# A fused attention and mixer kernel: float32 first tiles, another order of the opening, and four GpSimd sums per unit

## The chip, the core and the metric

The kernel runs on one core of a Trainium2 chip. The metric is the time of one execution on the device, in microseconds (us). Engines are named as in the profile: PE is TensorE, PEld its weight loads, DVE VectorE, ACT ScalarE, POOL GpSimd, SP the engine that issues the DMAs. "L615" is line 615 of the kernel before.

## What is computed

The input x has 2048 rows of 512 numbers. It is normalized, and the result goes two ways: through a sliding, dilated attention (32 heads of 16 numbers; each position looks at itself and at the seven positions 2, 4, ... 14 rows back), and through a two-layer network with GELU, whose output passes SiLU. The product of the two ways is added to x:

```python
xn = _layernorm(x)
qkv = (xn @ wqkv)                      # q, k, v: 32 heads of 16
idx = pos[:, None] - 2 * arange(8)     # window of 8, dilation 2
logits = einsum("bhsd,bhswd->bhsw", q, k[idx]) * 16 ** -0.5   # idx < 0 masked
s = einsum("bhsw,bhswd->bhsd", softmax(logits), v[idx]) @ wo
y = _layernorm(xn)
g = silu(gelu(y @ w1 + b1) @ w2 + b2)  # w1 512 x 1376, w2 1376 x 512
out = x + s * g
```

All is float32 in and out.

## The kernel before

**Layout.** Even and odd rows never meet in the attention (dilation 2), so they are two classes (c = 0, 1) of 1024 rows, each in eight tiles of 128 rows. A class has four blocks of eight heads (hb = 0 to 3). That makes eight units u of attention, in the order c = 0 with hb 0 to 3, then c = 1.

**Precision.** A float32 matrix product is made of three fp16 ones: each operand is scaled by a power of two and split into a high part and a low part (what the rounding left), and high x high, low x high and high x low are summed in PSUM. The scale comes from a sum of squares of the weights (ScalarE with accumulation, L458 for wqkv and L376 for w1 and wo; a matmul with a tile of fours sums it over the partitions, L384 or L389, `total`; VectorE makes the power of two from the exponent, L402 to L413). The high part is ScalarE's (L476, L429) or VectorE's (L427), the low part VectorE's (L478, L430).

**Opening (`ln0`, L531; `prep_q`, L453).** The even tiles are loaded in the order of `LOADS` (tiles 2, 3, then the first weight block in two DMAs, "q0" and "q2", then 0-1, 4-5, 6-7), normalized (statistics on VectorE L518, a power on GpSimd L505 and L512, the scaling on VectorE L554 or ScalarE L527), transposed on TensorE (L561) into PSUM, and split from there into yT (high on ScalarE L565, low on VectorE L566). Sixteen matmuls on constants (L1000, the count is `WAKE`) fill gaps of TensorE behind the first normalized tile.

**Projection (`qkv`, L595).** Per unit eight tiles of 12 fp16 matmuls (L615) into one of two PSUM buffers "ps"; ScalarE evicts each (L623) with its row scale (cs) into the unit's tile U[u % 2], which holds q, k and v of eight tiles plus copied halo rows of k and v (DMAs, L632 and L638). U is double-buffered over units, so the projections of unit u + 1 write where unit u - 1 was.

**Attention (`attention`, L651), VectorE above all.** Four products of q with shifted k (L666, 128 x 2048 each, into a ring of three buffers "prod"), each followed by a reduction over the 16 numbers of a head (L669); softmax (L689 to L697, exp on ScalarE L692); four products of the weights with shifted v (L722). The PV products acc, p1, p2, p3 are summed: two VectorE additions of 2048 (acc + p1, acc + p2, L717), then three GpSimd additions of 1024 (`beside`, L742), which are handed over in the list `pend` and taken out in the next unit's loop over the q-k products, at n = 1, 2 and 3. Each has a one-element copy ahead (L745) that waits for a q-k product, so that the addition (L746) runs beside the reduction of it. Then the result is split into fp16 (L705, L707), transposed by DMA (L710) into oT.

**Network (`mlp1`, L848; `mlp2`, L892).** 44 steps (four chunks of 512 rows x 11 blocks of w1): 12 matmuls (L856), GELU on ScalarE (L873), the high part on ScalarE (L876). The low part is VectorE's (L879) for steps in `DVE_LO` (8 to 43); for steps 0 to 7 a matmul with a negative diagonal subtracts the high part in PSUM (L885) and ScalarE reads the rest (L888). Two steps later 12 matmuls with w2 (L901) add to four z buffers.

**End (`wo_first` L796, `wo_last` L814).** Output projections (L792): for odd rows nine matmuls per tile over the first three head blocks, three more when the last block's oT is there; then the scaling and product with g (L836), the addition of x (L783 on VectorE, L785 on GpSimd) and the store (L786).

**Order.** Nothing runs in the order in which the code names it. Every operation goes into a list with an estimated duration, its reads and writes and a priority (`Plan.add`); `Plan.issue` (L201) plays the engines through with these estimates and so fixes each engine's order; the engines then execute in that order and wait on semaphores. DMAs are modelled with a rate, an issue time and a tail; up to the time `SLOW` a lower rate is taken. `port=True` marks operations that the plan lets use the port that VectorE and GpSimd share only one after the other. Lower priority numbers go first: projections of unit u have 1000 u, network steps 1000000 and above, so the network fills what the projections leave. `qkv(u + 1)` is put on the list ahead of `attention(u)` (L1135 to L1139).

## Time and profile before

| what | value |
|---|---|
| median of three runs (lowest to highest) | 424.1 us (423.76 to 425.4) |
| the profiled execution | 424.13 us |
| its span in the trace | 422.4 us |
| TensorE busy, matmuls | 408.6 us, 2098 |
| VectorE busy | 391.8 us |
| ScalarE busy | 215.7 us |
| GpSimd busy | 78.2 us |
| first projection matmul (L615) | 11.8 us |
| first network matmul (L856) | 49.9 us |
| end of the last matmul | 417.8 us |

The execution's own time is longer than the span by 1.7 us, which lie around it. A line of the timeline gives the start, the length of a merged group, engine, line, operation and tiles, the count, and in brackets the idle time before it with what ended it. A line of the stretches gives, for each engine, the busy time and the number of instructions in parentheses, then the granted TensorE clock, the share of the DMA engines and GB/s.

### The profile page before, as it was taken

To read this page: it belongs to the slowest core of one execution; us is meant where nothing else is said; L and a number is where in the kernel's file an instruction comes from. 1 tells how busy PE (TensorE), PEld (TensorE's weight loads), DVE (VectorE), ACT (ScalarE), POOL (GpSimd) and SP (SyncE) were. 2 spreads that over 40 slices of the span, in tenths; PEclk is the share of its full clock that TensorE was granted. 3 is DMA by queue.
4 is the path that set the end of the run, shared out by engine and by line. 5 is a ranking of instruction groups with operands and counts; after the bars stand their busy time and mean duration, and the time that the engine had idled before them with its cause. 6 is when DMAs were issued, how large, how long until landed. Compare 5 with 4: busy or idle time off the path is not lost.

```text
span 422.4 us, 5540 instructions
## 1 busy us (share of the span) xinstructions
PE 408.6 (97%) x2098; PEld 208.2 (49%) x2098; DVE 391.8 (93%) x400; ACT 215.7 (51%) x325; POOL 78.2 (19%) x119
## 2 busy tenths in 40 slices
PE   4999989999999999999999999999999999999995
PEld 3565534445644564445544554455545554444442
DVE  4985999999998999999999999998999989999974
ACT  3899974872477754833375352234230492236400
POOL 5310200000450023202500240052002500250022
PEclk9999999999999999999999999999999999999999
DMA  7964260120044347430262022110425374007142
GB/s 259 415 267 137 69 218 2 67 82 2 1 122 166 68 102 170 92 58 2 72 164 100 0 88 50 52 66 36 136 75 175 74 219 143 2 0 222 37 138 101
DMA packets 42506, 44.83 MB, mean 106 GB/s; under 512 B 27464, under 2 KB 27648, under 8 KB 41968
## 3 DMA queue, kind: packets, MB, share of 16 engines
q1 hardware_dynamic: 42480, 44.49, 34.7%
q8 instruction: 16, 0.26, 0.2%
q14 instruction: 10, 0.08, 0.1%
HBM read 23.53 MB, written 7.34 MB: 73 GB/s over the span
## 4 chain that ended last, share of the span: by engine, by line
PE 85%; DVE 6%; ACT 4%; DMA 3%; issue 1%; SPq 0%; POOL 0%; DVEq 0%
PE z L901 27%; PE mh L856 25%; PE ps L615 22%; PE ps L792 6%; PE z L792 2%; DVE w L430 2%; DMA prod<-in_A_wqkv_dram 1%; PE mh L792 1%; DMA yT<-in_A_wqkv_dram 1%; DVE bn L518 1%; ACT w L376 1%; DMA U<-U 1%; ACT wq L458 1%; ACT U L623 1%; ACT yT L565 1%
## 5 line engine op out<-in xcount | busy, mean ns | idle before, releaser
L615 PE MATMUL ps<-wq,yT 128*128 128x384 f16 x768 | 130.0, 326 | 0.7 <-ACT U L623 0.7
L856 PE MATMUL mh<-yT,w 128*128 128x512 f16 (+1 forms) x528 | 121.3, 379 | 0.1
L901 PE MATMUL z<-w,h 128*128 128x512 f16 x480 | 111.5, 379 | 0.0
L615 PEld LDWEIGHTS <-yT 128*128 128x128 f16 x768 | 75.1, 98 | 52.2 <-issue 2.1
L856 PEld LDWEIGHTS <-w 128*128 128x128 f16 (+1 forms) x528 | 52.8, 100 | 60.9 <-issue 0.4
L873 ACT ACTIVATE mh<-mh,b1T,hsc 128x512 f32<-128x512 f32 (+1 forms) x44 | 33.0, 750 | 89.9 <-PE mh L856 89.8
L666 DVE TENSOR_TENSOR prod<-U 128x2048 f32<-128x2048 f32 x32 | 73.0, 2287 | 1.1 <-DMA U<-U 0.4
L901 PEld LDWEIGHTS <-h 128*128 128x128 f16 x480 | 47.0, 98 | 54.8
L669 DVE TENSOR_REDUCE L<-prod 128x128 f32<-128x2048 f32 x32 | 72.8, 2280 | 0.2
L623 ACT ACTIVATE U<-ps,cs 128x384 f32<-128x384 f32 x64 | 37.0, 583 | 64.3 <-PE ps L615 64.1
L722 DVE TENSOR_TENSOR prod<-L,U 128x2048 f32<-128x2048 f32 x28 | 63.1, 2284 | 0.2
L745 POOL COPY gate<-prod 1x1 f32<-1x1 f32 x21 | 4.4, 212 | 242.1 <-DVE prod L666 210.0
L717 DVE TENSOR_TENSOR prod<-prod,prod 128x2048 f32<-128x2048 f32 x16 | 36.5, 2284 | 0.0
L746 POOL TENSOR_TENSOR prod<-prod 128x1024 f32<-128x1024 f32 x14 | 32.9, 2351 | 0.0
L792 PEld LDWEIGHTS <-oT 128*128 128x128 f16 x192 | 18.8, 98 | 22.6
L876 ACT ACTIVATE h<-mh,hsc 128x512 f16<-128x512 f32 x40 | 27.5, 686 | 0.9
L792 PE MATMUL ps<-wo,oT 128*128 128x512 f16 x120 | 27.2, 379 | 0.0
L879 DVE SCALAR_TENSOR_TENSOR h<-mh,hsc,h 128x512 f16<-128x512 f32 x32 | 23.7, 742 | 2.3 <-ACT h L876 2.3
L746 POOL TENSOR_TENSOR prod<-prod,prod 128x1024 f32<-128x1024 f32 x7 | 16.4, 2348 | 0.0
L705 ACT ACTIVATE o<-prod,osc 128x1024 f16<-128x1024 f32 (+1 forms) x9 | 9.5, 1051 | 11.3 <-POOL prod L746 5.8
L873 ACT ACT_TABLE_LOAD x10 | 12.8, 1283 | 0.2
L561 PE MATMUL z<-ident,f 128*128 128x128 f32 x32 | 6.0, 318 | 6.6 <-DVE f L554 5.9
(146 smaller groups left out, 332.8 us busy)
## 6 DMA issues: line engine op xcount, KB each, us to landing
f<-in_A_x_dram SPq DMA_DIRECT2D x31, 256.0 KB, 4.4
U<-U SPq DMA_DIRECT2D x16, 392.0 KB, 3.6
gd<-f SPq DMA_DIRECT2D x12, 256.0 KB, 2.5
oT<-in_B_w_dram SPq DMA_DIRECT2D x2, 1024.0 KB
yT<-in_B_w_dram SPq DMA_DIRECT2D x2, 1024.0 KB, 13.3
f<-gd SPq DMA_DIRECT2D x8, 256.0 KB, 3.2
out_dram<-f SPq DMA_DIRECT2D x8, 256.0 KB, 2.1
out_dram<-U SPq DMA_DIRECT2D x8, 256.0 KB, 2.0
```

Of the source, the lines that this page charges most:

```text
L615: nc.tensor.matmul(b.t[:, 0:384], y[:, s, k, o:o + P], wq[:, hb, t, k], start=(n == 0), stop=(n == 11))
L623: act(384, lambda i=i, b=b: nc.scalar.activation(U3[:, i:i + 31:15, :], b.t[:, 0:384].rearrange("p (t e) -> p t e", t=3), AF.Identity, sca ...
L666: dve(2048, lambda p2=p2, g=g: nc.vector.tensor_tensor(p2(), q, slots(Ut, KH, 2 * g), op=ALU.mult), qk + [("kh", ub, 0), ("kh", ub, 1), (" ...
L669: dve(2048, lambda pr=pr, g=g: nc.vector.tensor_reduce(L3()[:, 2 * g:2 * g + 2], pr.t.rearrange("p (r f d) -> p r f d", r=2, d=DH), AX.X, ...
L717: dve(n, lambda: nc.vector.tensor_tensor(d(), a(), b(), op=ALU.add), keys, [dkey])
L722: dve(2048, lambda: nc.vector.tensor_tensor(pr.t.rearrange("p (r f d) -> p r f d", r=2, d=DH), L3()[:, 2 * g:2 * g + 2].rearrange("p r (f ...
L746: nc.gpsimd.tensor_tensor(x.t[:, 0:1024], x.t[:, 0:1024], y(), op=ALU.add)
L792: nc.tensor.matmul(b.t, oT[:, hb, i // 4, s, i % 4], wo[:, t, hb], start=(hb == 0 and n == 0), stop=(hb == NHB - 1 and n == 2))
L856: nc.tensor.matmul(b.t[0:M], w1[:, s, k, f * P:f * P + M], yT[ch][:, t, k], start=(n == 0), stop=(n == 11))
L873: act(512, lambda: nc.scalar.activation(b.t[0:M], b.t[0:M], AF.Gelu_apprx_tanh, bias=b1T[0:M, f:f + 1], scale=hsc[0:M, 1:2]), [b, ("b1T",) ...
L876: act(512, lambda: nc.scalar.activation(hi()[0:M], b.t[0:M], AF.Identity, scale=hsc[0:M, 2:3]), [b], [hk])
L901: nc.tensor.matmul(z.t, hl[s][0:K, t * P:(t + 1) * P], w2[0:K, w, f], start=(f == 0 and n == 0), stop=(f == NF - 1 and n == 2))
```

## The change

- **Loads.** Tile 3 is loaded after the first weight block in place of before it.
- **Float32 first tiles.** For tiles 2 and 3 (`FP`) of unit 0, ScalarE first copies the transposed tile from PSUM to a float32 tile yF. The projection of these two tiles is four float32 matmuls of 384 columns on yF and the raw weights, in place of twelve fp16 ones; the row scale loses the weight scale. The fp16 high and low parts, which other units and the network read, are made from yF at a lower priority.
- **PSUM.** In unit 0, and for the first four tiles of unit 1, every second projection tile takes a buffer of the ring "mh".
- **Idle matmuls.** 22 without any input, and 4 behind the first normalized tile, in the buffer z0, in place of 16 in "mh".
- **PV sums (units 0 to 6).** The third PV product is written over the unit's own q and k slots (the first 2048 columns of U). VectorE adds only its first half to acc (1024 in place of 2048); the second half is added on GpSimd to p3, by a fourth `beside` entry. The four entries are taken out at n = 0, 1, 2 and 3 of the next unit.
- **Order of the list.** `qkv(u + 1)` is put on the list inside `attention(u)`, after its first q-k product and the first GpSimd addition (`mid`), since it overwrites the tile that this addition reads.
- **Network.** `DVE_LO` begins at step 4, so steps 4 to 7 lose the subtraction matmul and ScalarE's L888 and get VectorE's L879.
- **End.** The last tile's three matmuls, scaling, addition and store are done in two halves of 256 columns; its addition moves no engine (VectorE).
- **Estimates of the planner.** `SLOW` 5.5 for 7.8; a tail of 3.5 for the DMAs of weight blocks 2 and 3 (1.4 before); priorities `PQLO` and `PFP`; GpSimd's additions 2.2 for 2.45; the powers on GpSimd without the port.

```diff
-LOADS = [(2, 1), (3, 1), "q0", "q2", (0, 2), (4, 2), (6, 2)]
+LOADS = [(2, 1), "q0", "q2", (3, 1), (0, 2), (4, 2), (6, 2)]
+FP = (2, 3)
-DVE_LO = range(8, 44)
+DVE_LO = range(4, 44)
-SLOW = 7.8
+SLOW = 5.5
-WAKE = 16
+WAKE = 4
+WAKE0 = 22
-PQLO = 0.45
+PQLO = 0.55
+PFP = 0.62
+U1MH = 4
...
     def k0(hb):
-        return dict(rate=400e3, tail=0.6, issue=0.45) if hb == 0 else {}
+        return dict(rate=400e3, tail=0.6, issue=0.45) if hb == 0 else dict(tail=3.5) if hb > 1 else {}
...
-            act(512, lambda p3=p3, hi=hi: nc.scalar.copy(hi, p3()), [b], [("yh", 0, i)], aps=0, **way)
+            if i in FP:
+                yf = yF[i] = R_L.new()
+                act(512, lambda b=b, yf=yf: nc.scalar.copy(yf.t, b.t), [b], [yf], aps=0, **way)
+                p3, b, way2 = (lambda yf=yf: yf.t.rearrange("p (k t) -> p k t", k=KT)), yf, dict(prio=PFP)
+            else:
+                way2 = way
+            act(512, lambda p3=p3, hi=hi: nc.scalar.copy(hi, p3()), [b], [("yh", 0, i)], aps=0, **way2)
             dve(512, lambda p3=p3, hi=hi, lo=lo: nc.vector.tensor_tensor(
-                lo, p3(), hi, op=ALU.subtract), [b, ("yh", 0, i)], [("y", 0, i)], port=False, **way)
+                lo, p3(), hi, op=ALU.subtract), [b, ("yh", 0, i)], [("y", 0, i)], port=i in FP, **way2)
...
-        for i in IORD if u else IORD0:
+        for n, i in enumerate(IORD if u else IORD0):
+            more = n % 2 and (u == 0 or u == 1 and n < U1MH)
...
-            b = R_ps.new()
+            b = (R_mh if more else R_ps).new()
...
-            ends = [1, 2, 3, 4, 8, 12] if u == 0 and i == IORD0[0] else [4, 8, 12] if u < 2 else [12]
+            ends = [4, 8, 12] if u < 2 else [12]
+            if u == 0 and i in FP:
+                yf = yF[i]
+                for k in range(KT):
+                    pe(1, 384, lambda k=k, b=b, yf=yf: nc.tensor.matmul(
+                        b.t[:, 0:384], yf.t[:, k * P:(k + 1) * P], stq[hb]()[:, k * 384:(k + 1) * 384],
+                        start=(k == 0), stop=(k == KT - 1)), [yf, ("stq", hb, k)], [b], fp32=4.1,
+                       holds=stkey[hb], after=pl.users([b] + [("v", ub, i)]))
+                ends = []
...
-            if pend and n:
+            if pend:
                 pend.pop(0)(pr)
                 if n == 3:
                     pend.pop(0)()
+            if n == 0:
+                mid()
...
             acc = pv(0)
             p1 = pv(1)
-            p2 = pv(2)
-            addto(acc, p1)
+            pv(2, p2t)
+            add(2048, lambda: acc.t, lambda: p1.t, lambda: acc.t, [acc, p1], acc)
             p3 = pv(3)
-            addto(acc, p2)
+            add(1024, lambda: acc.t[:, 0:1024], lambda: p2t[:, 0:1024], lambda: acc.t[:, 0:1024], [acc] + qkk, acc)
...
-            pend.extend([beside(acc, lambda: acc.t[:, 1024:2048]),
-                         beside(p3, lambda: p3.t[:, 1024:2048]),
-                         beside(acc, lambda: p3.t[:, 0:1024]), rest])
+            pend.extend([beside(p3, lambda: p2t[:, 1024:2048], qkk),
+                         beside(acc, lambda: acc.t[:, 1024:2048], []),
+                         beside(p3, lambda: p3.t[:, 1024:2048], []),
+                         beside(acc, lambda: p3.t[:, 0:1024], []), rest])
...
+            if i == NI - 1:
+                for h in range(2):
+                    cols = slice(h * 256, h * 256 + 256)
...
-    for _ in range(WAKE):
-        b = R_mh.new()
+    for n in range(WAKE0 + WAKE):
+        b = R_z[0].new()
         pl.add("pe", 0.2, lambda b=b: nc.tensor.matmul(b.t[:, 0:2 * P], idle[:, 0:P], idle, start=True,
-                                                       stop=True), [("yd", 2)], [b], prio=1e9)
+                                                       stop=True), [("yd", 2)] if n >= WAKE0 else [], [b], prio=1e9)
...
-        if 2 <= u + 1 < len(units):
-            with prio(PR_U * (u + 1)):
-                qkv(*units[u + 1], u + 1)
+        def mid():
+            if 2 <= u + 1 < len(units):
+                with prio(PR_U * (u + 1)):
+                    qkv(*units[u + 1], u + 1)
         with prio(PR_U * (u + 1) + 500):
-            attention(c, hb, u)
+            attention(c, hb, u, mid)
```

## The prediction

> **What bounds the kernel now.** I read the busy row of each engine, then the chain of work that ended last, then the waits, then the stretches. First the page, then four stretches of the span (TensorE's columns are the first after the length):
>
> ```profile
> PE 408.6 (97%) x2098; PEld 208.2 (49%) x2098; DVE 391.8 (93%) x400; ACT 215.7 (51%) x325; POOL 78.2 (19%) x119
> ...
> PE 85%; DVE 6%; ACT 4%; DMA 3%; issue 1%; SPq 0%; POOL 0%; DVEq 0%
> ```
>
> ```profile
> 0.00:11.80 11.80, 5.79 (x27) 4.53 (x28) 6.43 (x28) 4.57 (x9) 5.58 (x16) 1.00 0.80 276
> 11.80:49.90 38.10, 36.66 (x229) 22.25 (x227) 31.08 (x81) 36.32 (x67) 7.32 (x7) 1.00 0.57 214
> 49.90:60.10 10.20, 8.53 (x40) 3.61 (x37) 10.20 (x12) 6.75 (x12) 0.00 (x0) 1.00 0.86 281
> 60.10:417.80 357.70, 357.62 (x1806) 177.78 (x1806) 342.68 (x281) 168.10 (x241) 65.28 (x96) 1.00 0.30 84
> ```
>
> From 60.1 us to 417.8 us TensorE is busy 357.62 of 357.70 us. In that stretch the end moves only if TensorE is given less work or starts it sooner; time taken off VectorE, ScalarE or GpSimd there is worth nothing by itself. What can be won lies ahead of 60 us (no projection before 11.8 us, then 1.4 and 1.7 us of idle), and in the 4.6 us behind the last matmul.
>
> TensorE's timeline of the opening and of its one long wait:
>
> ```profile
> 5.88 1.12 PE L561 MATMUL z<-ident,f 128*128 128x128 f32 x4 [5.88 <-DVE f L554]
> 6.79 1.06 PE L1000 MATMUL mh<-fours 128*128 128x256 bf16 x4
> ...
> 12.36 2.89 PE L615 MATMUL ps<-wq,yT 128*128 128x384 f16 x15
> 15.55 0.66 PE L561 MATMUL z<-ident,f 128*128 128x128 f32 x4 [0.31 <-ACT f L527]
> ...
> 57.75 0.81 PE L856 MATMUL mh<-yT,w 128*128 128x512 f16 x3
> 60.14 0.38 PE L384 MATMUL ps<-s,fours 128*128 128x1 f32 x2 [1.58 <-ACT wq L458]
> ```
>
> The first projection matmuls wait for the prepared fp16 weights: ScalarE's sum of squares starts at 6.99 us, when the raw weights land, the scale comes from VectorE at 10.6 us, the first fp16 weights after that. At 58.5 us TensorE's queue holds the "total" of the third weight block (L384), whose data landed only at 59.1 us; TensorE stands for 1.58 us behind it while gelu tiles for L901 are ready (ScalarE finished the first at 55.5 us).
>
> **The change, part by part.** All is counted against the profiled execution: 424.13 us, of which the span is 422.4; its median over three runs is 424.1 us, so the two agree.
>
> *Float32 first tiles.* Tiles 2 and 3 of the first unit lose 24 fp16 matmuls and get 8 fp32 ones that read the raw weights. An fp16 matmul of 384 columns costs 1.95/12 = 0.1625 us (the chain's "1.95 PE ps L615 x12"), so the old 24 cost 3.9 us, and their evictions ended at 19.1 us. For an fp32 matmul of this size there is no row. Bounds: as fast as fp16, 0.65 us a tile; or the slow transposes at 5.88 us, 1.12/4 = 0.28 us for 128 columns, three times that for 384 and four of them, 3.4 us. I take the fp32 transposes once TensorE is at speed (0.66/4 for 128 columns): 2.0 us a tile. Either way they run while TensorE had nothing to do but idle matmuls (L1000), so only a late end would cost. They can start when the fp32 copy of the transposed tile is out: transposes end near 6.5, the raw weights land near 6.4 (their DMAs now stand one 0.43 us issue earlier, ahead of tile 3's), ScalarE first does a 0.94 us sum, then the copy (0.48): about 7.9 us. Tile 3 now lands behind the weights (near 7 us), its normalization, transposes and copy take it to about 11, so both tiles are done near 13.5 us instead of 18.4. That is 4.9 us at most.
> The Trainium skill ("FP8 and Floating Point Precision", "TensorE Precision Notes") says that true FP32 is four passes through the array. Worked out from the row of fp16, that is an estimate of 4 x 4 x 0.1625 = 2.6 us a tile; the sum would stay the same, since tile 3 arrives later than that. No row here shows an fp32 matmul of this size.
>
> How much of the 4.9 us stays? Behind it lie two chains. Tiles 0, 1, 4 to 7 still come from VectorE and ScalarE (their transposes run from 15.6 to 24.9 us), so TensorE would be fed too late unless those move up, too. And ScalarE is 36.3 of 38.1 us busy: it gets two copies more (2 x 0.48 = 0.96 us), and loses waits of 1.52, 1.00, 0.28 and 0.21 us and some 0.5 us at its first weights. That gives 2.5 us, plus 1.2 us of waits at 52.2 to 54.9 us. On the other side, the w1 weights leave VectorE at 48.9 us, just where TensorE begins L856 (49.9 us), but two mlp tiles need only the last quarter of theirs from the last pieces, so 18 matmuls of 0.216 us (3.9 us) can be done ahead. Bounds 0 and 4.9 us; I take 3.0, near the ScalarE row. A loss would need ScalarE's 0.96 us with no wait given back: 1 us.
>
> *22 idle matmuls from the start.* They need only the fours tile (1.0 us); at 1.06/4 each they end near 6 us at the latest. They are in front of the first transposes at 5.88 us, so they cost at most 0.2 us, and save up to 0.46 (1.12 against 0.66). Counted within the 3.0.
>
> *Later tail (3.5 us) for the third and fourth weight blocks in the planner's list.* It puts the L384 totals later, where the data has landed. The 1.58 us go, since L901 is ready; what is next late is the w2 pieces on VectorE (L430, the first done at 51.4 us), with 7 us in hand. I take 1.6. It could be 0 (another placement waits as long).
>
> *Four fewer subtraction matmuls* (steps 4 to 7): 4 x 0.216 = 0.9 us of TensorE in its full stretch. VectorE gets four L879 of 0.742, 3.0 us; ScalarE loses four L888. Each result has two steps of 5.2 us before L901 reads it, and VectorE's longest single instruction ahead of it is 2.28 us, so nothing waits.
>
> *Third PV product over q and k, four sums on GpSimd.* Per unit (seven units) VectorE does a 1024 add (1.22) in place of a 2048 one (2.28), 1.07 us less, 7.5 us in all; net of the 3.0 above 4.5 us less. TensorE sets the end, so that is worth 0. GpSimd gets seven more pairs of copy (0.17) and add (2.35), 2.52 us each, and it is 19% busy. The added wait: the next but one unit's evictions (L623) overwrite q and k, so they now wait for the first GpSimd add, which ends some 3.6 to 6 us later than the last PV product that they waited for before. Queued behind such an eviction on ScalarE are gelu and hi copies, and TensorE waits for those. The planner starts the projections after that add, and mlp work fills the time; but it counts 2.2 us for what takes 2.52. 7 x 0.32 = 2.2 us at worst, 0 if ScalarE's waits swallow it (it is half idle there). I take 0.8. The evictions need 15.6 us of a unit of about 40, so VectorE still gets its q and k in time.
>
> *The last tile in two halves.* Behind the last matmul stand L836 (0.75), L783 (0.69) and the store. With halves the second L836 and L783 take by the slope of rows (1.22 - 0.68 for 512 elements more) about 0.45 and 0.41, the first half's lie partly before; the store is half as large. 0.2 to 0.8 us, I take 0.4. TensorE's columns stay the same.
>
> **Sum:** 3.0 + 1.6 + 0.9 + 0.4 - 0.8 = 5.1 us; 424.1 - 5.1 = **419.0 us**.
>
> **The rivals.**
> *A, the whole opening gain* (4.9 us, and no eviction waits): 4.9 + 1.6 + 0.9 + 0.4 = 7.8, 416.3 us. For it: TensorE's early idle. Against: ScalarE's 95%.
> *B, the gain is hidden anyway:* tiles 0 to 7 and w1 come no sooner, so the opening gives 0, and evictions cost the full 2.2: 1.6 + 0.9 + 0.4 - 2.2 = 0.7, 423.4 us. For it: VectorE is 100% busy from 49.9 to 60.1 us and ScalarE full before.
> *C, slower: GpSimd's extra add collides with VectorE.* The rows of the old case:
>
> ```profile
> 197.99 2.29 DVE L669 TENSOR_REDUCE L<-prod 128x128 f32<-128x2048 f32 x1
> ...
> 198.22 2.34 POOL L746 TENSOR_TENSOR prod<-prod 128x1024 f32<-128x1024 f32 x1
> ...
> 200.38 2.34 DVE L666 TENSOR_TENSOR prod<-U 128x2048 f32<-128x2048 f32 x1
> ```
>
> GpSimd's adds lie beside a reduction, and the product that starts in the last 0.18 us of one took 2.34 us against a median of 2.284: a hint that they block each other. The new first add is released as soon as the PV sums are done. In units whose first q-k product was done early (in four of seven, at 76.2, 161.6, 212.5 and 252.2 us) it meets two-input products, not a reduction. If VectorE stood for every new add, it would lose 7 x 2.35 = 16.5 us, in all 16.5 + 3.0 - 7.5 = 12.0 us more work. VectorE's slack is 5.6 us: the last transposed output leaves at 405.3, lands 4.3 us later, and TensorE must have it after 36 matmuls from 407.4 us, at 415.2. So the end would move by 12.0 - 5.6 - 1.5 (earlier opening) = 4.9 us to 429.0. It decides from (5.6 + 4.5 + 1.5)/7 = 1.7 us lost per unit. Against it: the product already queued on VectorE starts first, and the add then falls beside the reduction behind it.
> The Trainium skill ("SBUF — State Buffer", "Who interferes with whom") states such a lock for the whole instruction between a VectorE instruction with two SBUF inputs and a reading GpSimd one, and none for a reduction. By that rule whoever starts first wins; the trace's 0.06 us agrees with its direction, and no row here shows the full price.
>
> **Chances.** The forecast (417 to 421.2) 0.52, A and below 0.10, B 0.23, C 0.15. The range must leave out C's most and a little below A: 416.0 to 424.5 us. About 0.5% (2.1 us) is what a measurement of this kernel can tell from no change. Faster, under 422.0: 0.52 + 0.10 + 0.06 of B = 0.68; same: 0.18; slower: 0.14.
>
> **What would show it.** Right: L615 in fp32 near 8 us; L856 starting at 46 to 47.5 us instead of 49.9; no 1.58 us at L384; four L885 instead of eight; TensorE full from then to about 413; about 4.2 us behind the last matmul. A: L856 at 45. B: L856 at 49 or later, or TensorE idle in front of L615 with ScalarE waiting for GpSimd. C: products (L666, L722) clearly above 2.3 us or VectorE idle beside GpSimd, and TensorE waiting for the last unit's output. Wrong altogether: the planner's new order leaves a wait of microseconds on TensorE that no row of before has.

## The result and the profile after

The changed kernel takes 428.21 us (median of six runs, 426.83 to 429.67) where the kernel before took 425.21 us beside it (six runs, 423.76 to 426.89). The ratio is 1.0087, with a 95% interval of 1.0062 to 1.0111: slower by 0.9%. The forecast was 419.0 us with a range to 424.5, so it failed in sign and in range. The profiled execution took 428.65 us against 424.13, its span is 426.86 us against 422.35.

First the busy rows and the engines' shares of the chain that ended last, then four stretches (us, then busy time and count of TensorE, its weight loads, VectorE, ScalarE and GpSimd, then granted TensorE clock, DMA share, GB/s):

```profile
PE 412.6 (97%) x2099; PEld 210.3 (49%) x2099; DVE 395.5 (93%) x406; ACT 217.4 (51%) x325; POOL 104.2 (24%) x133
...
PE 65%; DVE 23%; issue 5%; ACT 2%; DMA 2%; POOL 2%; SPq 1%; DVEq 0%; ACTq 0%
```

```profile
0.00:11.80 11.80, 8.68 (x36) 5.79 (x37) 6.41 (x27) 6.37 (x11) 6.06 (x16) 0.86 0.84 295
11.80:49.60 37.80, 35.99 (x223) 22.42 (x222) 29.84 (x78) 35.38 (x64) 7.36 (x7) 1.00 0.52 195
49.60:60.10 10.50, 10.37 (x50) 4.63 (x48) 10.50 (x12) 7.86 (x13) 0.00 (x0) 1.00 0.82 251
60.10:422.40 362.30, 357.56 (x1797) 177.49 (x1795) 347.24 (x288) 167.81 (x239) 90.82 (x110) 1.00 0.30 85
```

Before, TensorE stood for 0.08 us of the long stretch; now it stands for 362.30 - 357.56 = 4.74 us. The chain says the same: TensorE's share falls from 85% to 65%, VectorE's rises from 6% to 23%. The stretch from 49.6 us on shows one thing that came as forecast: TensorE is busy 10.37 of 10.50 us (before 8.53 of 10.20), the 1.58 us behind L384 (now L391) are gone.

TensorE's timeline has the opening and the two long waits (in brackets the idle time ahead and what ended it; from three stretches: the opening, the network's start, and 140 us on):

```profile
5.99 0.66 PE L571 MATMUL z<-ident,f 128*128 128x128 f32 x4 [1.19 <-DVE f L564]
...
8.13 3.61 PE L639 MATMUL ps<-prod,L 128*128 128x384 f32 x6
...
12.85 2.85 PE L639 MATMUL mh<-prod,L 128*128 128x384 f32 x8
...
49.64 4.70 PE L905 MATMUL mh<-yT,w 128*128 128x512 f16 x21
...
154.89 5.36 PE L632 MATMUL ps<-wq,yT 128*128 128x384 f16 x32 [2.42 <-ACT U L648]
...
198.75 4.42 PE L632 MATMUL ps<-wq,yT 128*128 128x384 f16 x16 [2.09 <-ACT U L648]
```

The float32 projections (L639) start at 8.13 us, but the first network matmul starts at 49.64 us, only 0.27 us earlier than before. Later TensorE waits twice for ScalarE's evictions (L648). The last line holds a second thing: 16 matmuls of 384 columns take 4.42 us, where at 0.1625 us each they would take 2.6.

**First wait.** GpSimd's power for class 1 (one number for each row, on 128 x 8) in the kernel before, then all engines of the changed kernel around 150 us:

```profile
125.46 1.64 POOL L512 TENSOR_TENSOR cT<-lw,halves 128x8 f32<-128x8 f32 x1
```

```profile
150.07 2.29 DVE L691 TENSOR_TENSOR prod<-U 128x2048 f32<-128x2048 f32 x1
150.24 3.62 POOL L519 TENSOR_TENSOR cT<-lw,halves 128x8 f32<-128x8 f32 x1 [1.44 <-DVE lw L518]
...
153.88 0.49 ACT L615 ACTIVATE cs<-cT,qsc 128x8 f32<-128x8 f32 x2 [4.70 <-POOL cT L519]
...
154.28 0.56 ACT L648 ACTIVATE U<-ps,cs 128x384 f32<-128x384 f32 x1
```

Two things changed. The power (now L519) comes 25 us later, at a place where evictions of a projection follow its row scale on ScalarE; and it starts beside a VectorE product of two SBUF tiles and takes 3.62 us in place of 1.64. ScalarE's row scale (L615) stands 4.70 us for it, the evictions stand behind L615 in ScalarE's queue, and TensorE's buffers stay full.

**Second wait.** All engines around 196 us, behind the copy that was to hold the sum back:

```profile
169.84 0.17 POOL L774 COPY gate<-prod 1x1 f32<-1x1 f32 x1 [2.95 <-DVE prod L691]
...
192.59 4.06 PE L632 MATMUL ps<-wq,yT 128*128 128x384 f16 x24
...
193.98 2.35 POOL L775 TENSOR_TENSOR prod<-prod,U 128x1024 f32<-128x1024 f32 x1 [23.97 <-DVE prod L750]
194.43 2.46 DVE L602 TENSOR_TENSOR f<-f,f 128x512 f16<-128x512 f32 x1
...
196.81 1.21 DVE L744 TENSOR_TENSOR prod<-prod,U 128x1024 f32<-128x1024 f32 x1
...
198.12 1.05 ACT L648 ACTIVATE U<-ps,cs 128x384 f32<-128x384 f32 x2 [2.43 <-DVE prod L744]
198.61 0.67 DVE L602 TENSOR_TENSOR f<-f,f 128x512 f16<-128x512 f32 x1
```

The new first GpSimd sum (L775, the form that reads U) starts as soon as the last PV product is done. Its gate copy (L774) had run at 169.84 us already, behind a q-k product that the plan had hoisted, so it no longer put the sum beside a reduction. VectorE's subtraction L602 (0.67 us at 198.61) takes 2.46 us beside it, the addition L744 behind it comes late, and the eviction that may overwrite q and k only after L744 stands 2.43 us. TensorE had begun the projections at 192.59 us, so its two buffers were full. Here it is VectorE that started later and stood.

The first sums of all seven units meet a two-input instruction of VectorE in this way, mostly L744, the addition of the other half: four sums take 3.13 to 3.22 us in place of 2.35, and beside the other three L744 takes 2.98 us (twice, in place of 1.22) or L602 its 2.46. Only the one at 194 us made TensorE wait for more than 0.2 us.

After this second wait the clock falls, as four windows show (same columns as the stretches):

```profile
8.00:11.00 3.00, 3.00 (x7) 1.79 (x7) 2.69 (x15) 2.60 (x6) 1.57 (x2) 0.50 1.08 422
151.00:155.00 4.00, 1.57 (x11) 0.88 (x9) 3.86 (x3) 1.11 (x5) 4.00 (x3) 1.00 0.01 2
196.00:198.00 2.00, 0.66 (x5) 0.29 (x3) 2.00 (x3) 0.00 (x0) 0.34 (x1) 1.00 0.00 0
199.00:202.00 3.00, 3.00 (x11) 1.42 (x10) 2.97 (x3) 0.17 (x1) 0.45 (x2) 0.50 0.78 93
```

From 198.74 to 202.16 us the granted clock is 0.50. The same happened from 7.59 to 11.01 us, on top of the float32 tiles. The mean granted clock of the six runs differed: the one at 1.0 took 426.83 us, the five from 0.985 to 0.999 took 427.74 to 429.67, so a part of the 3 us is not in every run.

**Accounting.** Take for each matmul the distance to the next one's start, less what its kind takes in the full stretches (0.1625 us for 384 columns, 0.216 for 512): what is left is time lost. At 70 us the changed kernel is 2.05 us ahead (344.96 us of TensorE's work left against 347.0). Behind that it loses 7.18 us, the kernel before 0.28: 2.59 at the first wait, 2.26 at the second, about 1.6 to the half clock, the rest in pieces under 0.2. -2.05 + 6.90 = +4.85; the last matmul ends 4.68 us later (422.44 against 417.76). Behind it 4.42 us against 4.59.

### The profile page after: what moved, and what is told of

Read it like the earlier page. It is cut to its first block, busy times and chain, and to the rows that moved or that the text cites. A ratio compares the mean times of both kernels' runs of the same rounds, so it can differ in the third digit from the quotient of the medians.

```text
span 426.9 us, 5571 instructions
## 1 busy us (share of the span) xinstructions
PE 412.6 (97%) x2099; PEld 210.3 (49%) x2099; DVE 395.5 (93%) x406; ACT 217.4 (51%) x325; POOL 104.2 (24%) x133
## 4 chain that ended last, share of the span: by engine, by line
PE 65%; DVE 23%; issue 5%; ACT 2%; DMA 2%; POOL 2%; SPq 1%; DVEq 0%; ACTq 0%
PE z L950 19%; PE ps L632 17%; PE mh L905 17%; PE ps L822 6%; DVE L L694 3%; DVE prod L691 3%; DVE prod L750 3%; PE z L822 2%; DVE w L437 2%; DVE prod L744 2%; DVE h L928 1%; PE mh L632 1%; DVE bn L525 1%; DMA prod<-in_A_x_dram 1%; PE mh L822 1%
## 5 line engine op out<-in xcount | busy, mean ns | idle before, releaser
L632 PE MATMUL ps<-wq,yT 128*128 128x384 f16 x684 | 116.4, 329 | 5.5 <-ACT U L648 4.5
L950 PE MATMUL z<-w,h 128*128 128x512 f16 x480 | 110.6, 379 | 0.0
L632 PEld LDWEIGHTS <-yT 128*128 128x128 f16 x744 | 73.2, 99 | 55.3 <-issue 6.7
L691 DVE TENSOR_TENSOR prod<-U 128x2048 f32<-128x2048 f32 x32 | 76.2, 2386 | 2.1 <-DMA U<-U 1.0
L950 PEld LDWEIGHTS <-h 128*128 128x128 f16 x480 | 47.0, 98 | 55.5
L694 DVE TENSOR_REDUCE L<-prod 128x128 f32<-128x2048 f32 x32 | 72.8, 2279 | 0.4
L648 ACT ACTIVATE U<-ps,cs 128x384 f32<-128x384 f32 x58 | 33.4, 578 | 65.1 <-PE ps L632 56.0
L775 POOL TENSOR_TENSOR prod<-prod,U 128x1024 f32<-128x1024 f32 x7 | 19.8, 2833 | 125.1 <-DVE prod L750 98.1
L750 DVE TENSOR_TENSOR prod<-L,U 128x2048 f32<-128x2048 f32 x21 | 47.7, 2284 | 0.1
L775 POOL TENSOR_TENSOR prod<-prod 128x1024 f32<-128x1024 f32 x14 | 32.9, 2349 | 0.0
L774 POOL COPY gate<-prod 1x1 f32<-1x1 f32 x28 | 7.9, 281 | 89.3 <-DVE prod L691 87.1
L928 DVE SCALAR_TENSOR_TENSOR h<-mh,hsc,h 128x512 f16<-128x512 f32 x36 | 26.7, 744 | 0.8 <-ACT h L925 0.8
L744 DVE TENSOR_TENSOR prod<-prod,prod 128x2048 f32<-128x2048 f32 x9 | 20.5, 2283 | 0.0
L732 ACT ACTIVATE o<-prod,osc 128x1024 f16<-128x1024 f32 (+1 forms) x9 | 9.5, 1054 | 18.0 <-POOL prod L775 12.8
L775 POOL TENSOR_TENSOR prod<-prod,prod 128x1024 f32<-128x1024 f32 x7 | 16.4, 2347 | 0.0
L750 DVE TENSOR_TENSOR U<-L,U 128x2048 f32<-128x2048 f32 x7 | 16.0, 2283 | 0.0
```

The source lines that it names most:

```text
L632: nc.tensor.matmul(b.t[:, 0:384], y[:, s, k, o:o + P], wq[:, hb, t, k], start=(n == 0), stop=(n == 11))
L648: act(384, lambda i=i, b=b: nc.scalar.activation(U3[:, i:i + 31:15, :], b.t[:, 0:384].rearrange("p (t e) -> p t e", t=3), AF.Identity, sca ...
L691: dve(2048, lambda p2=p2, g=g: nc.vector.tensor_tensor(p2(), q, slots(Ut, KH, 2 * g), op=ALU.mult), qk + [("kh", ub, 0), ("kh", ub, 1), (" ...
L694: dve(2048, lambda pr=pr, g=g: nc.vector.tensor_reduce(L3()[:, 2 * g:2 * g + 2], pr.t.rearrange("p (r f d) -> p r f d", r=2, d=DH), AX.X, ...
L744: dve(n, lambda: nc.vector.tensor_tensor(d(), a(), b(), op=ALU.add), keys, [dkey])
L750: dve(2048, lambda: nc.vector.tensor_tensor(dst().rearrange("p (r f d) -> p r f d", r=2, d=DH), L3()[:, 2 * g:2 * g + 2].rearrange("p r (f ...
```

## The experiments

Each ratio is against the kernel before on the same chip. "Lost" is time lost after 70 us as defined above; "network" is the start of the first network matmul (before: 49.91 us).

| kernel | median us | ratio, 95% interval | network | lost |
|---|---|---|---|---|
| before | 425.21 | 1 | 49.91 | 0.28 |
| changed | 428.21 | 1.0087, 1.0062 to 1.0111 | 49.64 | 7.18 |
| e1_open | 421.74 | 0.9937, 0.9913 to 0.996 | 48.50 | 1.01 |
| e2_pv | 425.06 | 1.003, 1.0012 to 1.0048 | 49.87 | 1.48 |
| e3_nopv | 422.47 | 0.996, 0.9943 to 0.9978 | 48.76 | 2.26 |
| e4_port | 423.73 | 0.9991, 0.9968 to 1.0013 | 46.69 | 4.02 |
| e5_late | 422.46 | 0.9963, 0.9947 to 0.9979 | 48.69 | 2.23 |
| e7_best | 423.02 | 0.998, 0.996 to 1.0001 | 48.97 | 0.42 |
| e8_port | 424.39 | 1.0007, 0.9989 to 1.0025 | 50.83 | 0.45 |
| e10_nogate | 439.07 | 1.0353, 1.0308 to 1.0397 | 49.50 | 15.3 |
| e9_late2 | 423.15 | 0.9969, 0.9959 to 0.9979 | 49.71 | 2.26 |
| e11_late_port | 420.81 | 0.9925, 0.9897 to 0.9954 | 46.64 | 1.98 |
| e12_pv_late | 425.32 | 1.0026, 1.0004 to 1.0049 | 50.79 | 0.88 |
| e13_open_end | 420.2 | 0.9926, 0.9893 to 0.9959 | 46.16 | 1.01 |

### Which part loses the time

**e1_open**: the kernel before with the opening (loads, float32 tiles, idle matmuls, "mh" for units 0 and 1, their estimates) and the tail of weight blocks 2 and 3.

```diff
+FP = (2, 3)
+WAKE0 = 22
...
+        return dict(rate=400e3, tail=0.6, issue=0.45) if hb == 0 else dict(tail=3.5) if hb > 1 else {}
```

> The kernel before with the opening part alone (load order, float32 first tiles, buffers, idle matmuls, the longer DMA tail); no change to the PV sums, the powers' port flag, the subtraction matmuls or the end. In the kernel after, TensorE was about 2.0 us ahead at 70 us and lost 6.5 us later, in two waits (2.6 us at 152 us, 2.3 us at 196 us) and a half clock behind the second (1.6 us). Theory, collisions of GpSimd's new work with VectorE's two-input instructions: this kernel keeps the gain and has no such waits, 1.2 to 2.0 us faster than before. Rival, the opening's new order itself leaves the later stages badly placed (class 1 statistics late): TensorE waits at 140 to 200 us here too, 1 to 4 us slower than before.

Measured 0.9937. The opening and the tail are a gain of some 2.2 to 2.7 us (2.2 by the medians, 2.7 by the ratio), even though in its profile the first four float32 instructions start 0.64 us or more apart (0.32 in the kernels at full speed), and the network starts at 48.50. Its one wait behind 70 us is 0.73 us at 82 us: no wait at 140 to 200 us, as the theory said, and a gain a little above its 1.2 to 2.0 us.

**e2_pv**: the kernel before with the PV part alone (third product over q and k, four GpSimd sums, `mid`).

```diff
-            if pend and n:
+            if pend:
                 pend.pop(0)(pr)
...
+            pv(2, p2t)
```

> The kernel before with the PV part alone: third PV product over q and k, fourth GpSimd sum, projections listed in the middle of attention. Theory, collisions: TensorE waits of 2 us and more at the projections of some units, and possibly a half clock behind them; 2 to 6 us slower than before. Rival, the loss comes from the reordered opening or the port flag: within 1 us of before, with TensorE full from 60 us to the end.

Measured 1.003: the PV part by itself costs 0.3%, 1.3 us, which is less than the theory's 2 us and more than the rival's 1. Its first sums take 2.83 us in the mean where the other sums take 2.35, so they collide here too; TensorE loses 1.12 us once, at 313 us. A power on GpSimd took 3.63 us in this kernel, although the flag is on: the plan keeps powers and products apart by its estimates only.

**e3_nopv**: the changed kernel without the PV part.

```diff
-            pv(2, p2t)
+            p2 = pv(2)
...
+            addto(acc, p2)
```

> The kernel after without the PV part (sums as before). Theory, collisions of the new sum: 2 to 3.5 us faster than before (about 2.0 at 70 us, 0.2 at the end, and what is left of the four subtraction matmuls), TensorE full from 70 us on. Rival, the port flag of the powers or the new order: a wait of 2 us or more at the projections of unit 3 or 4 stays, and the time is equal to before or slower.

Measured 0.996, so most of the loss goes with the PV part: 1.0087 to 0.996 is 5.4 us of 425. But its median is not below that of e1_open, which holds fewer gains (the intervals overlap). One of its powers still collides, the one for class 1's rows (by-form group, mean ns behind the busy time); the one for the row scales takes 1.65 us:

```profile
L512 POOL TENSOR_TENSOR lw<-lw,halves 128x8 f32<-128x8 f32 x1 | 3.7, 3682 | 9.1 <-DVE lw L504 9.1
```

TensorE's longest wait behind 70 us, 1.50 us up to 135.93 us, is not for a power: it waits for a low part on VectorE (L923) that stood behind two PV products. And the network starts at 48.76 us though its float32 instructions ran at full speed, 0.323 us each. That pointed at an edit that the prediction had passed over, the powers' flag.

**e4_port**: the changed kernel with the flag restored.

```diff
-            rb.t[:, 0:n], p0b.t[:, 0:n], halves[:, 0:n], op=ALU.pow), [p0b], [(rb, 0)], prio=pp, port=False)
+            rb.t[:, 0:n], p0b.t[:, 0:n], halves[:, 0:n], op=ALU.pow), [p0b], [(rb, 0)], prio=pp)
...
-            cdst, a1(), halves[:, 8:8 + n], op=ALU.pow), [(A, 1)], ckeys, port=False)
+            cdst, a1(), halves[:, 8:8 + n], op=ALU.pow), [(A, 1)], ckeys)
```

> The kernel after with the port flag of the normalization's powers restored, so that the planner again keeps them apart from VectorE's two-input instructions. In the kernel after, the class 1 power took 3.62 us beside a product (1.64 before), ScalarE stood 4.7 us behind it and TensorE 2.6 us. If the flag is that cause: no wait at 152 us, 2 to 3 us faster than after. If the new sums alone do it: another wait takes its place, within 1 us of after.

Measured 0.9991, 1% better than the changed kernel. Two lines of its by-form groups:

```profile
L775 POOL TENSOR_TENSOR prod<-prod,U 128x1024 f32<-128x1024 f32 x7 | 20.2, 2890 | 114.8 <-DVE prod L750 114.8
...
L519 POOL TENSOR_TENSOR cT<-lw,halves 128x8 f32<-128x8 f32 x1 | 1.6, 1645 | 3.1 <-DVE lw L518 3.1
```

The power is back at 1.65 us, it runs at 124.61 us in place of 150.24, and the wait at 152 us is gone. The first sums collide as before (2.89 us), and TensorE now waits at 232, 272, 347 and 383 us (0.51, 1.37, 0.38 and 1.33). The surprise is the opening: the network starts at 46.69 us. VectorE's timeline shows why. The statistics of the first of tiles 0 and 1 are the third L525; first the changed kernel, then e4_port:

```profile
9.69 0.68 DVE L582 TENSOR_TENSOR yT<-L,yT 128x512 f16<-128x512 f32 x1
...
10.98 0.62 DVE L485 SCALAR_TENSOR_TENSOR wq<-prod,qsc,wq 128x384 f16<-128x384 f32 x1
11.52 0.69 DVE L525 BATCH_NORM_STATS2 bn<-prod 128x6 f32<-128x512 f32 x1
```

```profile
9.04 0.54 DVE L564 TENSOR_SCALAR f<-prod,lw,lw 128x512 f32<-128x512 f32 x1
9.49 0.69 DVE L525 BATCH_NORM_STATS2 bn<-prod 128x6 f32<-128x512 f32 x1
```

Without the flag the plan thinks that VectorE's subtractions L582 and L485 fit beside the power and puts them ahead of tile 0's statistics; with it the statistics come first, 2.03 us sooner, and all the tiles behind follow. Not all of the 2.03 us is the order: tile 3 landed 0.65 us sooner in this profile (the second L525 starts at 6.88 against 7.53 us), which leaves 1.38. The same order stands in all kernels with the float32 tiles: L582 and L485 ahead of the third L525 where the flag is off (e3_nopv, e9_late2), behind it where it is on (e1_open, e7_best, e11_late_port).

**e8_port**: the kernel before with the flag off and nothing else (the same two lines, reversed).

> The kernel before with the port flag of the normalization's powers taken away, nothing else. Theory, the flag lets the planner put a power beside a two-input VectorE instruction: the class 1 powers (1.64 us) take up to 3.7 us; if ScalarE's row scales stand behind one, TensorE waits 1 to 2.5 us, 0 to 3 us slower. Rival, the flag only does harm together with the new sums: within 1 us of before.

Measured 1.0007, no difference, though a power took 3.68 us in it. That is the one for class 1's rows (L505). The one for the row scales (L512) moved from 125.46 to 146.40 us, but took 1.65, and ScalarE stood 1.30 us for it; TensorE lost 0.45 us in all. So the flag costs nothing by itself: late as this power was, without a collision it hardly held TensorE.

### What the first GpSimd sum costs

**e5_late**: the changed kernel, with the first q-k product of a unit held back until the last PV product of the unit before is issued, as the other three already are.

```diff
-            late = last[-1:] if n else []
+            late = last[-1:]
```

In this kernel one part of the work is changed: the loads of g for the end overwrite columns of U[0] that the first GpSimd sum of unit 6 still reads, so that sum adds other numbers. The amount of work is the same, but that sum waited 3.33 us for the DMA and took 3.82.

> The kernel after, in which the next unit's first q-k product also waits for the last PV product, as the other three do; the first GpSimd sum's gate then opens beside a reduction instead of long before. In the kernel after the gate of unit 3's first sum opened at 169.8 us, the sum ran at 194.0 us beside a two-input VectorE instruction that took 2.46 us instead of 0.69, and TensorE waited 2.3 us. Theory, collision of the first sum: the first sums take 2.35 us instead of 2.83 on average and the wait at 196 us is gone; the wait behind the class 1 power (152 us) may stay; 1 to 4 us faster than after. Rival, what holds TensorE is the planner's order and not the collision: first sums at 2.35 us, but as slow as after or slower, since VectorE loses its filler during the exp (1.1 to 1.5 us a unit).

Measured 0.9963 in place of 1.0087: 5.3 us. **e9_late2** is the same with the release of U[0] put behind unit 7, so that all is computed:

```diff
-            late = last[-1:] if n else []
+            late = last[-1:]
...
-        if u == 6:
+        if u == 7:
```

> The kernel after, in which the next unit's first q-k product also waits for the last PV product (first sum beside a reduction), and the end's loads into U[0] are released only after unit 7's attention, so that unit 6's first sum reads q and k's tile undisturbed. The run without the second edit was 5.7 us faster than after. Theory, collision of the first sum: 1.0 to 1.4% faster than after, 0.1 to 0.5% faster than before; first sums at about 2.4 us. Rival, that run was only faster because of the early loads at the end: within 0.4% of after.

Measured 0.9969. The first sums, by form:

```profile
L775 POOL TENSOR_TENSOR prod<-prod,U 128x1024 f32<-128x1024 f32 x7 | 16.5, 2357 | 0.0
```

All seven are at the undisturbed price (2357 ns against 2833), beside reductions. What is left of the loss is 2.26 us, most of it in waits of 0.70 us at 86 us and 0.79 at 269. The powers took 1.65 and 1.63 us in this order and ran at 127.77 and 129.40 us, by chance: the flag is still off. So the first wait is gone as well, as it was in e5_late, and this edit was not made for that: of the time that it gains, 2.6 us belong to that wait and not to the sums. The opening still starts the network at 49.71 us.

**e11_late_port**: e9_late2 with the flag restored as in e4_port.

> As the last one, and the powers' port flag restored. Theory, both collisions taken away: what the opening gives (0.6%) plus four subtraction matmuls (0.9 us), 0.6 to 1.0% faster than before, the best of the study. Rival, the two remedies take away the same waits, and VectorE's lost filler costs as much: like the run with late first products alone (0.1 to 0.5%).

Measured 0.9925 (420.81 us). The two repairs add up in part: 1.0087 goes to 0.9969 with the late product, to 0.9991 with the flag, to 0.9925 with both; 0.0118 + 0.0096 would give 0.9873, so they overlap by some 2 us, as they must where both remove the first wait. The network starts at 46.64 us, the last matmul ends at 413.63.

**e12_pv_late**: the kernel before with the PV part in its undisturbed form (e2_pv with the two edits of e9_late2).

> The kernel before with the PV part and both edits of the last two runs (first products late, loads at the end released later). The PV part alone was 0.3% slower. Theory: with the first sum beside a reduction nothing is lost, and as TensorE sets the end nothing is gained either: 0.1% slower to 0.2% faster than before. Rival, the wait of the evictions for the fourth sum costs by itself: still 0.3% slower.

Measured 1.0026. Its first sums take 2.355 us and its powers 1.65, and still it gains nothing: the 6.1 us by which VectorE is busy less (385.7 against 391.8) are not on the path. That it lies 0.26% above is not settled: 0.9 us of the 1.1 are there when the network starts (50.79 us), and the opening of e8_port, with another edit, was as late (50.83).

**e10_nogate**: the other way round, the kernel before with its three sums set free of their gate, and the plan not told of the port.

```diff
-                        nc.gpsimd.tensor_copy(gate, pr.t[0:1, 0:1])
...
-                    pool(2.45, fn, [acc, p3, pr], [x, ("gate",)], prio=p)
+                    pool(2.45, fn, [acc, p3], [x, ("gate",)], prio=p, port=False)
```

> The kernel before with the one-element copy and the wait for a q-k product taken from GpSimd's three sums, so that they run as soon as the PV sums are done, beside whatever VectorE does. It measures the collision by itself. If two-input VectorE instructions and GpSimd's sums shut each other out for a whole instruction: some of the 21 sums take 3 to 4.7 us instead of 2.35, or some products (2.28) and additions do; 1 to 2.4 us lost per unit; VectorE has 5.6 us of slack, so 0 to 8 us slower. If they share without loss: all sums at 2.35, all products at 2.28, the same time.

Measured 1.0353, 15 us slower, where 0 to 8 us were expected. Groups by form of the kernel before, then of this one, and one stretch of its timeline:

```profile
L666 DVE TENSOR_TENSOR prod<-U 128x2048 f32<-128x2048 f32 x32 | 73.0, 2287 | 1.1 <-DMA U<-U 0.4
L669 DVE TENSOR_REDUCE L<-prod 128x128 f32<-128x2048 f32 x32 | 72.8, 2280 | 0.2
...
L746 POOL TENSOR_TENSOR prod<-prod 128x1024 f32<-128x1024 f32 x14 | 32.9, 2351 | 0.0
...
L746 POOL TENSOR_TENSOR prod<-prod,prod 128x1024 f32<-128x1024 f32 x7 | 16.4, 2348 | 0.0
```

```profile
L666 DVE TENSOR_TENSOR prod<-U 128x2048 f32<-128x2048 f32 x32 | 85.2, 2667 | 0.3
L669 DVE TENSOR_REDUCE L<-prod 128x128 f32<-128x2048 f32 x32 | 72.9, 2283 | 0.5
L745 POOL TENSOR_TENSOR prod<-prod 128x1024 f32<-128x1024 f32 x14 | 46.3, 3324 | 166.1 <-DVE prod L717 134.6 <-issue 29.2 <-DVE prod L722 2.3
...
L745 POOL TENSOR_TENSOR prod<-prod,prod 128x1024 f32<-128x1024 f32 x7 | 26.5, 3783 | 0.0
```

```profile
101.44 6.73 POOL L745 TENSOR_TENSOR prod<-prod 128x1024 f32<-128x1024 f32 x2 [29.20 <-issue]
...
102.04 3.89 DVE L666 TENSOR_TENSOR prod<-U 128x2048 f32<-128x2048 f32 x1
```

This is the full price that the prediction had no row for. Two sums of 2.35 us, and a product of 2.28 that starts 0.6 us after the first of them, keep GpSimd for 6.73 us: 2.35 + 2.35 + 2.28 = 6.98, nearly one after the other. The product waits out the first sum, the second sum waits out the product. The reductions keep their 2.283 us (before 2.280): they don't collide. Three sums per unit cost TensorE 15 us here. VectorE's q-k products are 85.2 - 73.0 = 12.2 us longer in all, GpSimd's sums 72.8 - 49.3 = 23.5.

### Which version is best

**e7_best**: the kernel before with the opening, the tail, the four subtraction matmuls fewer and the halves at the end; without the PV part, and with the flag on as in the kernel before (in the expectations of this run and the last one, "without the flag" is without the change to it).

```diff
-DVE_LO = range(8, 44)
+DVE_LO = range(4, 44)
...
```

> The kernel before with opening, longer tail, four fewer subtraction matmuls and the end in halves; without the PV part and without the port flag. Theory: the gains of the opening run (0.6%) plus four matmuls of 0.216 us and some 0.3 us at the end, 1 us more: 0.8 to 1.0% faster than before, the fastest of all. Rival, more VectorE work (3 us) without the PV part's saving makes VectorE late at the end: as fast as the opening alone or slower.

Measured 0.998: the theory missed, the rival holds. TensorE loses only 0.42 us and its last matmul ends at 414.56, but the end of the span comes 8.25 us later:

```profile
410.06 1.41 DVE L880 SCALAR_TENSOR_TENSOR U<-ps,osc,U 128x512 f32<-128x512 f32 x2 [2.86 <-PE ps L817]
...
413.75 0.82 PE L867 MATMUL z<-wo,oT 128*128 128x256 f16 x6
...
417.13 0.86 DVE L871 SCALAR_TENSOR_TENSOR U<-z,osc,U 128x256 f32<-128x256 f32 x2
...
417.91 1.25 DVE L874 TENSOR_TENSOR U<-U 128x256 f32<-128x256 f32 x2
```

VectorE runs without a pause from 410.06 us, and the last scaling (L871) starts 2.6 us behind its matmuls. The four low parts cost VectorE 3.0 us, and the PV part, which spared it 6.1 in e12_pv_late, is not there. In e11_late_port, which has both, 4.44 us lie behind the last matmul. That suggests that the PV part pays for the four matmuls, but it is not shown. e3_nopv differs from this kernel by the flag alone: it has the four low parts and no PV part, and yet its VectorE waits for the last matmuls:

```profile
403.50 0.75 DVE L732 SCALAR_TENSOR_TENSOR o<-prod,osc,o 128x512 f16<-128x512 f32 x1 [0.79 <-ACT o L730]
...
416.17 0.88 DVE L871 SCALAR_TENSOR_TENSOR U<-z,osc,U 128x256 f32<-128x256 f32 x2 [1.85 <-PE z L867]
```

There VectorE ends the attention (L732) at 404.25 us, in e7_best at 407.20, and 4.42 us lie behind the last matmul. So the order matters here, and not the amount of work alone; and between these two kernels the flag gains nothing (0.996 off, 0.998 on).

**e13_open_end**: e7_best with `DVE_LO` as before.

```diff
-DVE_LO = range(4, 44)
+DVE_LO = range(8, 44)
```

> The opening part, the longer tail and the end in halves, without the four fewer subtraction matmuls, the PV part and the flag. With the four of them VectorE came late at the end (last matmul at 414.6 us, span 422.8 us). Theory, VectorE is the engine that is late there: without its 3 us more work the tail is 4.2 to 4.6 us again, 0.5 to 0.8% faster than before. Rival, the halves themselves make the tail long: 0.2% or less faster, the tail over 6 us.

Measured 0.9926 (420.2 us, 419.26 to 422.92). It, e11_late_port and e1_open (0.9937) are the best three and can't be told apart; all beat both kernels. The network starts at 46.16 us, TensorE loses 1.01 us after 70 us, 4.43 us lie behind the last matmul. So the theory holds for the end: the halves don't make the tail long. Of the 5.3 us between the spans of e7_best and this one, though, 2.8 are there when the network starts, and e7_best's float32 tiles ran at half speed.

## Why the prediction was wrong

**The failed steps are two.** The first is the last line of the change's list, "the powers on GpSimd without the port". The prediction gave it no term at all, because it looked like an estimate of the planner. In the opening it put two instructions of VectorE ahead of the next tile's statistics: among the kernels whose float32 tiles ran at full speed the network starts at 48.76 us with the flag off (e3_nopv) and at 46.16 to 46.69 with it on. And it moved the class 1 power to 150.24 us, beside a product, which made the first wait (2.59 us). Taking it back gained 4.1 us on the changed kernel (e4_port) and 1.9 on e9_late2 (e11_late_port), but nothing on e3_nopv (e7_best), so its price hangs on the rest of the order. The second is the term "I take 0.8" for the new wait of the evictions. It counted only GpSimd's surplus over the planner's estimate, at most 2.2 us, and trusted that the projections start after the sum. Measured were 2.26 us at one eviction, in projections that had started before the sum, and 1.6 us of half clock behind it. Behind it stood a collision that the prediction had put into rival C and priced against VectorE's slack. Its last sign came true: "the planner's new order leaves a wait of microseconds on TensorE that no row of before has".

**Point by point.**

- *Opening, 3.0 us.* It gave 0.27 us in the changed kernel, 3.2 to 3.75 where the flag is on and the float32 tiles ran at full speed (e4_port, e11_late_port, e13_open_end), 0.9 to 1.4 with the flag on and half speed (e7_best, e1_open), 1.15 with the flag off and full speed (e3_nopv). The mechanism and its size were right; the flag and the clock undid it. The 22 idle matmuls ended at 4.81 us ("near 6 us at the latest" was only a bound), and TensorE then idled 1.19 us ahead of the first transposes; that this idle time is what the clock answered to is argued, not shown.
- *A float32 tile, 2.0 us.* A tile is a group of eight instructions (two for each matmul) of 0.323 us each at full speed, 2.6 us. The term was too small by 0.6 a tile, and that cost little, as the prediction said: both tiles were done at 13.2 to 14.0 us where the clock was full (e13_open_end, e11_late_port, e4_port, e3_nopv), against the 13.5 of the prediction. The 15.5 us of the changed kernel are the half clock. The Trainium skill ("FP8 and Floating Point Precision", "TensorE Precision Notes") says four passes; the trace agrees, 2 x 0.323 = 0.646 us for a matmul of 384 columns, four times the 0.1625 of fp16.
- *Tail of weight blocks, 1.6 us.* Right: the 1.58 us are gone, L950 starts at 58.13 us (L901 at 60.38).
- *Four matmuls fewer, 0.9 us.* Right for TensorE. That VectorE has room for the four low parts held in the changed kernel, e3_nopv and e11_late_port, and failed in e7_best (8.25 us behind the last matmul).
- *PV part, 0 us for VectorE's saving.* Right: 1.003 with collisions, 1.0026 without, so no gain either way. With collisions there is not even a saving: VectorE is busy 391.9 us in e2_pv, 391.8 before.
- *The last tile in halves, 0.4 us.* 0.17 us.
- *Rival C.* Its 429.0 us is near the measured time, but for another reason. The argument against it, "the product already queued on VectorE starts first, and the add then falls beside the reduction" failed: the sum was released by the last PV product, and what VectorE had next was a subtraction of class 1's rows. VectorE did not run out of its slack, as the rival had it; 4.42 us lie behind the last matmul. The few microseconds reached TensorE through ScalarE's queue, where an eviction stood behind the late instruction. The prediction's own row at 198.22 us had hinted at the lock; the question that it did not ask was which instruction stands behind the one that is held up.

The Trainium skill ("SBUF — State Buffer", "Who interferes with whom") says that a VectorE instruction with two SBUF inputs and a reading GpSimd instruction exclude each other for their whole length, that the one issued first goes first, and that reductions never take part. The trace agrees in all three: power 1.64 to 3.62 us, L602 0.67 to 2.46 us, reductions 2.283 against 2.280 us in e10_nogate.

**What stays open.** Why e12_pv_late is 0.26% slower; and why VectorE is late at the end of e7_best and not of e3_nopv. And the clock of the opening: in the profiles of e4_port, e11_late_port, e13_open_end and e3_nopv the float32 instructions ran at 0.323 us from the start, in those of the changed kernel, e1_open, e5_late, e7_best and e9_late2 four to seven of them started 0.64 us or more apart. In the first four TensorE idles for 0.24 to 1.03 us of the 3.41 us cell of the granted clock that begins at 5.0 to 6.8 us; in the changed kernel and e1_open it idles for 2.01 and 2.19 us of the cell from 4.18 and 4.91 us, and the next cell has half the clock. But in e5_late 1.31 us of idle time was enough, and the profiles of e7_best and e9_late2 have no record of full clock before 13.67 and 13.22 us, so idle time is not the whole of it. No run controlled it, so part of every difference between these kernels, up to some 2 us, is this.

## What to carry to other kernels

Every edit of a planner's table is an edit of the kernel: a flag or an estimate reorders queues, and has to be costed by asking which instructions change places and who stands behind them. A gate that puts an instruction beside a harmless neighbour holds only as long as the event it waits for lies where it used to; when work is hoisted past it, it is open too early. When two engines exclude each other, price it along the in-order queue behind the one held up, as far as the engine that bounds the kernel, and not by the slack of the one held up.

## What the runs showed of the hardware

- A tiny GpSimd instruction pays the lock in full: the power on 128 x 8 numbers took 3.62 to 3.68 us in place of 1.63 to 1.65, in the changed kernel and in e2_pv, e3_nopv, e8_port and e10_nogate.
- The records of the granted clock in the changed kernel begin and end at 4.18, 7.59, 11.01, 198.74 and 202.16 us. All lie on one grid of 3.413 us: (198.74 - 7.59) / 3.413 = 56.0. The idle 2.09 us at 196.66 lay within one of its cells and cost the next cell half the clock; the idle 2.42 us at 152.47 lay across the border at 154.37, 1.90 us of it in one cell, and cost nothing. In e10_nogate waits of 3.33 and 2.55 us left the matmuls behind them 0.161 to 0.163 us apart for 384 columns, full speed; on its grid they fall into two cells each (1.95 and 1.39 us, 1.82 and 0.73). The ends of two other kernels agree: 1.96 us in the cell from 414.68 us of e3_nopv cost nothing, 2.42 us in the cell from 416.00 us of e9_late2 halved the next. The Trainium skill ("TensorE: Matmul & The Clock Gate", Part 1) has this window, free-running and 3413 ns long; it says that a whole idle window lowers the clock, and here 2.09 us of one did. For cells of fp16 matmuls the limit lies between 1.96 and 2.09 us of idle time in these profiles; e5_late's 1.31 us in the opening, among short float32 matmuls, does not fit it.
